# First loads of a fused state-space and gated kernel in another order, with new instruction sequences

## The chip, the core and the metric

The kernel runs on one NeuronCore of a Trainium2 chip. The core has a matrix engine (PE, with its own record PEld for loading weights), a vector engine (DVE), a scalar engine (ACT), a general engine (POOL) and a queue engine (SP), which here issues every DMA. They run side by side and meet only at semaphores. The metric is the device time of one execution in microseconds (us), as the median of several runs; beside it stands one profiled execution with a record of every instruction.

## The reference

```python
def reference(A_u, A_log_A_real, A_A_imag, A_C_real, A_C_imag, A_log_dt, A_D_skip,
              B_x, B_w_gate, B_w_up, B_w_down, gate_w):
    x = A_u                                              # (1, 2048, 448)
    g = _sigmoid((x * gate_w).sum(-1, keepdims=True))
    a = _A_ref(x, ...)   # K = 2 Re(sum_n C P), y = causal convolution of x with K by FFT, + x * D_skip
    b = _B_ref(x, ...)   # (sigmoid(x w_gate) * (x w_up)) w_down, inner width 1792
    return g * a + (1 - g) * b
```

Both branches read the same 2048 tokens of 448 channels. Branch A builds a kernel K of 2048 taps for each channel from 256 complex modes and convolves with it. Branch B is a gated layer with two matrix products up to width 1792 and one down again.

## The kernel before

All work is written as a list of operations in `gated_mix`, each with an engine, operands and a key (engine, tile name, priority). The order on each engine is fixed by hand: the table `PLACE` (lines 28 to 342) gives for every key the positions that its operations take in their engine's sequence. `Plan.order` (line 565 on) merges the five sequences. Every engine then works strictly through its own list: an instruction that waits holds up everything behind it on that engine, and a DMA that waits for a buffer holds up every later DMA on SP.

The parts that matter here:

- **Wake-up.** `step_sizes` memsets a tile `ones` on DVE (L1026) and lets PE multiply it with itself 24 times (L1031, 48 passes in the record, tile `fps`), first of all on PE. Nothing reads the result.
- **Branch B, "GLU".** The tokens come in two halves H and each half in two blocks B of 512. `glu_x` loads a block in four DMAs of 256 KB: column halves z (256 tokens each) times pairs of row blocks k (0 for row blocks 0 and 1, 2 for row blocks 2 and 3). `glu_xk` issues one such DMA into a raw tile (`raw_tile`: 7 buffers `xr0` for the first half, 4 buffers `xr` later), lets ACT round it into `xs` (L1332), and lets DVE compute what rounding lost (L1336, or L1338 and L1339). `glu_w` does the same for the weights of one slice f of 128 gate and 128 up columns: two DMAs (k = 0 and 2), ACT to `wh` (L1365), DVE to `wl` (L1367). A raw buffer comes free when both have read it.
- `glu_mm` multiplies: for one slice f, one block and gate or up (g = 0, 1), 11 matmuls of 512 columns over row blocks 0 to 3 (L1400 to L1405). Row block 0 needs the k = 0 part of the weights and of **both** column halves of x. The result lies in one of two PSUM tiles `gu`. ACT takes the tanh of the gate tile (L1384), DVE multiplies it with the up tile (L1386, to `hh` or `hl`), and these two reads free the PSUM tiles. `glu_down` multiplies with the down weights (L1419, or L1421 to L1423 where the operands are split) and ACT (L1431) or DVE (L1438) adds the result to `ob`.
- **Prologue of branch A.** `step_sizes` and `params` load `x` (log_dt, 1.8 KB), `cr`, `ci`, `la`, `ai` and compute steps and phases, mostly on DVE (L985, L988, L991 are the helper lines).
- **Chunks of branch A.** `kgen` runs 28 chunks; for each, PE computes phases (`tp`, L1224, L1233), ACT takes sines and roundings of them (`cs`, `nn`, L1228 to L1246), DVE multiplies with powers (L1253, L1267, L1270) and PE contracts (`kp`, L1282). GLU matmuls lie between them on PE. Chunk 13 ends the first half of the channels; the same stretch loads the second half H = 1 of the tokens (`xs`, positions 4 to 7 of key ('Act', 'xs', 5)).
- **Convolution** (`Chain`): matmuls on parts of the array (L813, L846, L890, L927), their evacuations `fx` on ACT, and DMAs through DRAM.

The head of the list issues the first loads: `glu_x(0, 0, 0)` and then `glu_w(0, 0, 0)`, so x with all four parts, then the weights of slice 0.

Of the kernel before, what the change touches and what calls it, by code (L numbers as in the profile page):

```python
# [11 lines left out]
F32R = mybir.dt.float32r  # L12
# [16 lines left out]
    ('Act', 'aci', 10): (11, 39,),  # L29
    ('Act', 'aci', 19): (61, 88,),  # L30
    ('Act', 'acr', 10): (15, 37, 46,),
    ('Act', 'acr', 19): (63, 84, 98,),
# [26 lines left out]
    ('Act', 'dots', 1): (28,),  # L59
    ('Act', 'dots', 2): (50,),  # L60
    ('Act', 'dots', 16): (80, 81,),
# [642 lines left out]
def gated_mix(ctx: ExitStack, tc, u, ut, aim, cre, cim, ldt, dskip, gw,  # L704
# [19 lines left out]
    phd = dt_([6, D, N], "phd")  # L724
# [836 lines left out]
```

## Time and profile before

| | us |
|---|---|
| median of 3 runs | 693.52 (692.16 to 694.05) |
| the profiled execution | 693.17 |
| its span | 691.4 |

The span is the time between the first and the last record; 1.8 us of the profiled execution lie outside it. The page of the profile gives the busy time of each engine; a view by windows gives it for chosen stretches, with the granted clock of PE ("PEclk", 1.00 is the full level) and what the DMA engines did. The timeline lists instructions with their start, their duration and, in brackets, how long the engine had sat idle before and what ended that.

### The profile page before, as it was taken

How to read it: one execution, taken by the hardware profiler on the slowest of the kernel's cores; microseconds unless marked ns; L12 is line 12 of the kernel's file. 1: busy time of each engine (PE TensorE's matmuls, PEld its weight loads, DVE VectorE, ACT ScalarE, POOL GpSimd, SP SyncE). 2: the span in 40 equal slices, each digit the busy share in tenths (PEclk: the TensorE clock that was granted, in tenths of full speed). 3: DMA queues.
4: the chain of work that ended last, by engine and by line, in shares of the span. 5: the costliest groups of instructions: out<-in, count | busy, mean ns of one | idle time of the engine just before them, and what ended most of it. 6: DMA issues, size and time to landing. Idle time of an engine off the chain costs nothing.

```text
span 691.4 us, 16303 instructions
## 1 busy us (share of the span) xinstructions
PE 678.0 (98%) x6588; PEld 485.0 (70%) x6588; DVE 603.4 (87%) x705; ACT 513.7 (74%) x934; POOL 276.4 (40%) x280
## 2 busy tenths in 40 slices
PE   8999999999999999999999999999999999999996
PEld 7766667877876687675556667778878766556874
DVE  5999999999999999999999788999973479667976
ACT  5587799899999999999999999999942351342110
POOL 0215458556467758584665745758000000000000
PEclk9999999999999999998999999999999999999999
DMA  9768442646886784859966885355947973879966
GB/s 261 190 161 220 111 125 52 169 118 246 193 172 153 183 201 127 241 169 221 170 167 182 215 230 124 103 210 156 190 104 184 247 254 139 281 251 247 183 171 172
DMA packets 98771, 126.11 MB, mean 182 GB/s; under 512 B 31240, under 2 KB 81096, under 8 KB 97672
## 3 DMA queue, kind: packets, MB, share of 16 engines
q1 hardware_dynamic: 98696, 125.07, 69.2%
q8 instruction: 52, 0.85, 0.5%
q14 instruction: 23, 0.19, 0.1%
HBM read 81.46 MB, written 43.58 MB: 181 GB/s over the span
## 4 chain that ended last, share of the span: by engine, by line
PE 83%; ACT 9%; DVE 3%; DMA 2%; issue 1%; SPq 0%; ACTq 0%; DVEq 0%
PE gu_gps L1400 11%; PE gu_gps L1401 10%; PE gu_gps L1402 10%; PE dn_gps L1419 8%; PE kp_egp L1282 6%; PE dn_gps L1421 4%; PE tp_egp L1224 4%; PE dn_gps L1422 4%; PE dn_gps L1423 4%; PE tp_egp L1233 4%; PE fps_fups L813 3%; PE gu_gps L1404 3%; PE gu_gps L1405 3%; PE fps_fups L846 2%; PE fps_fups L890 2%; PE fps_fkps L890 2%
## 5 line engine op out<-in xcount | busy, mean ns | idle before, releaser
L1400 PE MATMUL gu_gps<-xs_glu,wh_glu 128*128 128x512 f32 x336 | 146.9, 437 | 0.4 <-DVE hh_glu L1386 0.3
L1401 PE MATMUL gu_gps<-xs_glu,wh_glu 128*128 128x512 f32 x336 | 132.4, 394 | 0.0
L1402 PE MATMUL gu_gps<-xs_glu,wl_glu 128*128 128x512 f32 x336 | 132.3, 394 | 0.0
L1270 DVE TENSOR_TENSOR cs_eg<-cs_eg,es_eg 128x2048 f32<-128x2048 f32 x56 | 130.3, 2326 | 1.3
L1214 POOL TENSOR_TENSOR tb_eg<-tb_eg 128x96 f32<-128x96 f32 (+2 forms) x84 | 115.0, 1372 | 5.9
L1253 DVE TENSOR_TENSOR es_eg<-tb_eg 128x1024 f32<-128x1024 f32 x112 | 111.4, 1016 | 2.2
L1400 PEld LDWEIGHTS gu_gps<-xs_glu,wh_glu 128*128 128x128 f32 x336 | 63.5, 189 | 29.7 <-issue 12.6
L1384 ACT ACTIVATE sg_glu<-gu_gps 128x512 f32<-128x512 f32 x56 | 34.0, 607 | 63.5 <-PE gu_gps L1405 60.4
L1267 DVE TENSOR_TENSOR cs_eg<-cs_eg,es_eg 128x1024 f32<-128x1024 f32 x56 | 70.6, 1260 | 10.9 <-ACT cs_eg L1246 7.7
L1230 ACT ACTIVATE nn_eg<-cs_eg 128x512 fp32r<-128x512 f32 x112 | 72.6, 648 | 6.0 <-PE tp_egp L1233 4.6
L1401 PEld LDWEIGHTS gu_gps<-xs_glu,wh_glu 128*128 128x128 f32 x336 | 63.6, 189 | 15.9 <-issue 5.6
L1402 PEld LDWEIGHTS gu_gps<-xs_glu,wl_glu 128*128 128x128 f32 x336 | 63.4, 189 | 15.0 <-DVE wl_glu L1367 0.5
L1217 POOL TENSOR_TENSOR tb_eg<-tb_eg,bs_eg 128x32 f32<-128x32 f32 x84 | 70.4, 841 | 5.8
L1228 ACT ACTIVATE cs_eg<-tp_egp 128x512 f32<-128x512 f32 x112 | 68.6, 618 | 3.2 <-DVE og L958 2.0
L1236 ACT ACTIVATE cs_eg<-tp_egp 128x512 f32<-128x512 f32 x112 | 68.4, 616 | 1.7 <-PE tp_egp L1233 1.5
L1235 ACT ACTIVATE cs_eg<-tp_egp 128x512 f32<-128x512 f32 x112 | 68.2, 618 | 1.5 <-PE tp_egp L1233 1.1
L1438 DVE SCALAR_TENSOR_TENSOR ob_glu<-dn_gps,og,ob_glu 128x448 f32<-128x448 f32 x72 | 48.7, 677 | 23.3 <-PE dn_gps L1423 21.3
L1246 ACT ACTIVATE cs_eg<-cs_eg,half_pi 128x1024 f32<-128x1024 f32 x56 | 66.1, 1180 | 0.5
L1204 POOL MEMSET tb_eg<- 128x96 f32 x28 | 7.8, 286 | 131.6 <-DVE es_eg L1253 124.2
L1282 PEld LDWEIGHTS kp_egp<-cs_eg 128*32 128x32 f32 x3584 | 51.3, 110 | 11.0 <-issue 8.6
L1282 PE MATMUL kp_egp<-cs_eg 128*32 128x64 f32 x3584 | 55.8, 220 | 0.1
L1421 PE MATMUL dn_gps<-vh_glu,hh_glu 128*128 128x448 f32 x136 | 52.3, 384 | 0.8 <-DVE ob_glu L1438 0.8
(161 smaller groups left out, 1338.7 us busy)
## 6 DMA issues: line engine op xcount, KB each, us to landing
shf<-fx_fu SPq DMA_DIRECT2D x16, 896.0 KB
fx_fu<-shf SPq DMA_DIRECT2D x16, 896.0 KB
us<-fx_fu SPq DMA_DIRECT2D x16, 896.0 KB
xr_glu<-in_w_dram SPq DMA_DIRECT2D x52, 256.0 KB
uax_fk<-us SPq DMA_DIRECT2D x16, 448.0 KB
ua_fk<-us SPq DMA_DIRECT2D x16, 448.0 KB
xr_glu<-in_w_dram SPq DMA_DIRECT2D x17, 224.0 KB
gt_pre<-in_u_dram SPq DMA_DIRECT2D x8, 448.0 KB
```

The lines of the kernel that those rows point to most:

```text
L1214: pool(96 * m, lambda n=n, m=m: G.tensor_mul(g3(n + 1, m), g3(1, m), g3(n, 1).to_broadcast([128, 32, 3, m])))
L1217: pool(32, lambda e=e: G.tensor_mul(t(e + 1), t(e), b(3)))
L1228: op("Act", c_act(512, True), lambda: S.activation(cs[:, 1, ds, 32:96], block(tp), AF.Copy, bias=MAGIC), [tp], [(cs, ("s", i))], prio)
L1230: op("Act", c_act(512), lambda: S.activation(block(nn), cs[:, 1, ds, 32:96], AF.Copy, scale=-1.0, bias=MAGIC), [(cs, ("s", i))], [nn], prio)
L1253: V.tensor_mul(o.rearrange("p d (i k) -> p d i k", k=ny), x.unsqueeze(3).to_broadcast([128, 16, nx, ny]), y.unsqueeze(2).to_broadcast([128 ...
L1267: op("DVE", c_dve(1024), lambda: V.tensor_mul(cs[:, :, :, 0:32], cs[:, ::-1, :, 63:31:-1], es[:, :, 0:32].unsqueeze(1).to_broadcast([128, ...
L1270: op("DVE", c_dve(2048), lambda: V.tensor_mul(cs[:, :, :, 32:96], cs[:, :, :, 32:96], es[:, :, 32:96].unsqueeze(1).to_broadcast([128, 2, 1 ...
L1282: T.matmul(kp[32 * j:32 * j + 32, q], cs[:, z, 4 * j + q, 64:96], cs[:, z, 4 * j + q, 0:64], start=cs is parts[0] and z == 0 and q == 0, s ...
L1400: T.matmul(p.real, wh[:, k, cs], x[:, k], start=(k == 0), stop=False)
L1401: T.matmul(p.real, wh[:, k, cs], x[:, 4 + k], start=False, stop=False)
L1402: T.matmul(p.real, wl[:, k, cs], x[:, k], start=False, stop=False)
L1421: T.matmul(p[:, :D], hh[:, ts], vh.real, start=(i == 0), stop=False)
```

## The change

It does two things.

First, `glu_x(0, 0, 0)` and `glu_w(0, 0, 0)` become `glu_first(0)`. The same six loads, with the same roundings behind them, come in the order: x of the first 256 tokens with row blocks 0 and 1; weights of slice 0, row blocks 0 and 1; x of the second 256 tokens, row blocks 0 and 1; then the same three for row blocks 2 and 3. `glu_w` is cut into a generator for that.

```diff
+    def glu_first(prio):
+        x = xs[0, 0] = glu.tile("xs", 2, (128, 7, 512), F32R)
+        parts = glu_w_parts(0, 0, prio)
+        for k in (0, 2):
+            glu_xk(x, k, 0, slice(0, 256), 0, prio)
+            next(parts)
+            glu_xk(x, k, 1, slice(256, 512), 256, prio)
+        for _ in parts:
+            pass
+
...
     def glu_w(H, f, prio):
+        for _ in glu_w_parts(H, f, prio):
+            pass
+
+    def glu_w_parts(H, f, prio):
         wh, wl = (glu.tile(t, WB, (128, 4, 256), F32R) for t in ("wh", "wl"))
...
             glu_split(wr, lambda wr=wr: wr.real, wh, wl, lambda t, k=k: t[:, k:k + 2], k, 512, prio, 7 * H + f // 2)
+            yield
         ws[H, f] = (wh, wl, vh, vl)
...
-    glu_x(0, 0, 0)
-    glu_w(0, 0, 0)
+    glu_first(0)
```

Second, the table `PLACE` is replaced: the sequences of PE, ACT, DVE and SP are new from end to end (POOL's stays). On PE no operation moves by more than 15 positions of 1043. The entries of the head that the text below speaks of:

```diff
-    ('DVE', 'hh', 5): (27, 47, 68, 94, 113,),
-    ('DVE', 'ones', 10): (1,),
-    ('DVE', 'phs', 20): (0,),
-    ('DVE', 'wl', 0): (6, 8,),
-    ('DVE', 'wl', 1): (9, 16,),
-    ('DVE', 'x', 10): (11,),
-    ('DVE', 'xs', 0): (2, 3, 5, 7,),
+    ('DVE', 'hh', 5): (21, 50, 69, 91, 113,),
+    ('DVE', 'ones', 10): (0,),
+    ('DVE', 'phs', 20): (95,),
+    ('DVE', 'wl', 0): (1, 5,),
+    ('DVE', 'wl', 1): (7, 8,),
+    ('DVE', 'x', 10): (10,),
+    ('DVE', 'xs', 0): (2, 3, 4, 6,),
...
-    ('SP', 'ai', 10): (28,),
-    ('SP', 'ci', 10): (6,),
-    ('SP', 'cr', 10): (10,),
-    ('SP', 'x', 10): (8,),
-    ('SP', 'xr0', 1): (7, 9,),
-    ('SP', 'xr0', 2): (11, 12, 14, 15,),
+    ('SP', 'ai', 10): (23,),
+    ('SP', 'ci', 10): (15,),
+    ('SP', 'cr', 10): (8,),
+    ('SP', 'x', 10): (9,),
+    ('SP', 'xr0', 1): (6, 7,),
+    ('SP', 'xr0', 2): (10, 11, 12, 13,),
```

In the PE sequence the first eight GLU steps of slice 0 now go g0 row blocks 0, 1, then g1 row block 0, then g0 row blocks 2, 3, then the rest of g1 (before: all of g0, then all of g1). Around chunk 13 the PE sequences read, from the contraction `kp` 13 to the first GLU step of the second half (`gu` 224):

```
before: kp13, tp116, tp118, dn98, dn99, fps22, tp117, tp119, fps23, tp120, gu224
after:  kp13, fps22, tp116, dn97, tp118, dn98, dn99, fps23, dn100, tp117, dn101, tp119, gu224
```

and `dn97` stands before `kp13` in the sequence before. On ACT the rounding `nn` 58, which `tp` 117 reads, stands 4 positions behind the evacuation of chunk 13 (`ke` 13) before and 9 behind it after; `nn` 59, which `tp` 119 reads, follows 3 positions behind `nn` 58 in both.

## Rows read from the trace of the kernel before

**Rows 1.** Page, part 1: busy us (share of the span) of each engine.

```profile
PE 678.0 (98%) x6588; PEld 485.0 (70%) x6588; DVE 603.4 (87%) x705; ACT 513.7 (74%) x934; POOL 276.4 (40%) x280
```

**Rows 2.** Windows: length, busy us of PE PEld DVE ACT POOL, PEclk, DMA, GB/s.

```profile
20.00:25.00 5.00, 5.00 (x23) 3.91 (x22) 5.00 (x9) 0.58 (x1) 0.00 (x0) 1.00 1.04 274
...
100.00:300.00 200.00, 199.25 (x2467) 149.52 (x2466) 196.47 (x189) 193.17 (x355) 128.05 (x122) 1.00 0.66 166
...
310.00:316.00 6.00, 4.54 (x19) 2.52 (x18) 5.99 (x8) 5.97 (x13) 0.00 (x0) 0.84 0.81 207
316.00:321.00 5.00, 5.00 (x12) 3.32 (x11) 4.97 (x6) 4.33 (x8) 2.71 (x4) 0.51 0.93 249
321.00:350.00 29.00, 27.19 (x388) 17.05 (x390) 27.50 (x25) 27.01 (x47) 20.18 (x19) 1.00 0.95 183
...
500.00:680.00 180.00, 179.56 (x1207) 124.23 (x1207) 128.40 (x161) 55.84 (x106) 0.00 (x0) 1.00 0.75 206
```

**Rows 3.** Windows, wake-up line L1031 alone: PE, PEld, PEclk, DMA share, GB/s.

```profile
1.60:6.80 5.20, 5.12 (x24) 5.12 (x25) 1.00 0.89 272
6.90:9.50 2.60, 2.60 (x25) 2.60 (x24) 1.00 1.06 313
```

**Rows 4.** Timeline of the first 17 us: start, duration, engine, line, operation [idle before].

```profile
0.91 0.48 DVE L1184 MEMSET phs<- 1x512 f32 x1 [0.91 <-PEq L1551]
1.46 0.17 DVE L1026 MEMSET ones_pro<- 112x128 f32 x1
...
1.68 8.10 PE L1031 MATMUL fps_fups<-ones_pro 112*128 112x128 f32 x48 [1.68 <-DVE ones_pro L1026]
...
5.76 0.63 ACT L1332 ACTIVATE xs_glu<-xr_pre 128x512 fp32r<-128x512 f32 x1 [0.97 <-DMA xr_pre<-in_ut_dram]
...
8.62 0.63 ACT L1365 ACTIVATE wh_glu<-xr_pre 128x512 fp32r<-128x512 f32 x1 [2.23 <-DMA xr_pre<-in_w_dram]
...
9.54 0.47 PE L1400 MATMUL gu_gps<-xs_glu,wh_glu 128*128 128x512 f32 x1
...
9.68 0.62 ACT L1365 ACTIVATE wh_glu<-xr_pre 128x512 fp32r<-128x512 f32 x1
...
10.34 0.42 DVE L1339 TENSOR_TENSOR xs_glu<-xr_pre,xs_glu 64x256 fp32r<-64x256 f32 x1
...
12.65 0.16 DVE L985 TENSOR_SCALAR xr_pro<-x_pro 112x4 f32<-112x4 f32 x1
...
13.02 0.39 PE L1400 MATMUL gu_gps<-xs_glu,wh_glu 128*128 128x512 f32 x1
...
14.83 0.39 PE L1400 MATMUL gu_gps<-xs_glu,wh_glu 128*128 128x512 f32 x1
...
15.88 0.69 DVE L1386 SCALAR_TENSOR_TENSOR hh_glu<-sg_glu,gu_gps 128x512 f32<-128x512 f32 x1
15.97 0.39 PE L1402 MATMUL gu_gps<-xs_glu,wl_glu 128*128 128x512 f32 x1
...
16.62 0.50 PE L1400 MATMUL gu_gps<-xs_glu,wh_glu 128*128 128x512 f32 x1 [0.27 <-DVE hh_glu L1386]
```

**Rows 5.** Timeline of PE around a step on a part of the array (L813).

```profile
141.93 1.03 PE L813 MATMUL fps_fups<-fx_fu,ft_fu 64*128 64x224 f32 x8
142.89 0.50 PE L1404 MATMUL gu_gps<-xs_glu,wh_glu 128*128 128x512 f32 x1
143.22 0.39 PE L1405 MATMUL gu_gps<-xs_glu,wl_glu 128*128 128x512 f32 x1
```

**Rows 6.** Timeline of PE around chunk 13.

```profile
312.88 0.50 PE L1233 MATMUL tp_egp<-nn_eg,idn 128*128 128x512 f32 x1 [1.00 <-ACT nn_eg L1230]
...
316.64 0.63 PE L1400 MATMUL gu_gps<-xs_glu,wh_glu 128*128 128x512 f32 x1
317.07 0.63 PE L1401 MATMUL gu_gps<-xs_glu,wh_glu 128*128 128x512 f32 x1
```

**Rows 7.** Chain of work that ended last, in order of time: start, us, what.

```profile
34.32 1.50 PE dn_gps L1419 x4
```

More of the change, by code (lines that the diff above doesn't have):

```diff
@@ L28 @@
 PLACE = {
[L29 to L32, printed above, removed]
[26 rows of a table removed]
-    ('Act', 'dots', 1): (28,),
-    ('Act', 'dots', 2): (50,),
-    ('Act', 'dots', 16): (80, 81,),
[15 rows of a table removed]
+    ('Act', 'aci', 10): (14, 37,),
+    ('Act', 'aci', 19): (63, 88,),
+    ('Act', 'acr', 10): (12, 35, 47,),
+    ('Act', 'acr', 19): (64, 84, 97,),
[26 rows of a table added]
+    ('Act', 'dots', 1): (29,),
+    ('Act', 'dots', 2): (48,),
+    ('Act', 'dots', 16): (65, 82,),
[15 rows of a table added]
         911, 914, 916,),
[2 rows of a table removed]
[2 rows of a table added]
     ('Act', 'idn', 10): (17,),
-    ('Act', 'junk', 10): (34, 59,),
-    ('Act', 'junk', 19): (76, 78, 113,),
[12 rows of a table removed]
-    ('Act', 'pos_sb', 10): (65, 74,),
[22 rows of a table removed]
-    ('DVE', 'aci', 10): (50,),
-    ('DVE', 'aci', 19): (105,),
-    ('DVE', 'acr', 10): (82,),
+    ('Act', 'junk', 10): (33, 59,),
+    ('Act', 'junk', 19): (75, 79, 114,),
[12 rows of a table added]
+    ('Act', 'pos_sb', 10): (69, 71,),
[22 rows of a table added]
+    ('DVE', 'aci', 10): (42,),
+    ('DVE', 'aci', 19): (110,),
+    ('DVE', 'acr', 10): (85,),
     ('DVE', 'acr', 19): (150,),
@@ L123 @@
     ('DVE', 'ai', 19): (145,),
[13 rows of a table removed]
-    ('DVE', 'dtp', 10): (40,),
-    ('DVE', 'dtv', 10): (26,),
[14 rows of a table removed]
-    ('DVE', 'half_pi', 0): (4,),
[21 rows of a table removed]
[13 rows of a table added]
+    ('DVE', 'dtp', 10): (44,),
+    ('DVE', 'dtv', 10): (32,),
[14 rows of a table added]
+    ('DVE', 'half_pi', 0): (25,),
[21 rows of a table added]
     ('DVE', 'og', 1): (52,),
     ('DVE', 'og', 2): (80,),
[1 row of a table removed]
-    ('DVE', 'ones', 10): (1,),
-    ('DVE', 'p', 10): (18, 20, 21, 22, 23, 24, 25,),
-    ('DVE', 'phs', 20): (0,),
[6 rows of a table removed]
-    ('DVE', 'skip', 20): (35,),
[6 rows of a table removed]
-    ('DVE', 'uax', 40): (540, 544, 551, 552, 567, 565, 576, 575, 582, 581, 588, 587, 594, 595, 600, 599, 629, 630,
[26 rows of a table removed]
[1 row of a table added]
+    ('DVE', 'ones', 10): (0,),
+    ('DVE', 'p', 10): (16, 18, 20, 24, 27, 28, 30,),
+    ('DVE', 'phs', 20): (95,),
[6 rows of a table added]
+    ('DVE', 'skip', 20): (13,),
[6 rows of a table added]
+    ('DVE', 'uax', 40): (544, 542, 550, 551, 567, 566, 576, 574, 579, 582, 588, 587, 594, 595, 598, 599, 629, 630,
[26 rows of a table added]
         1032, 1035, 1038, 1039, 1042,),
     ('PE', 'fps', -1): (0,),
[43 rows of a table removed]
[43 rows of a table added]
     ('Pool', 'bsx1', 10): (5, 11,),
```

494 rows, old and new, of the table PLACE are left out of this document.

## Prediction, made before the changed kernel was run

> **What bounds the kernel now.** I read the page first, then the windows, then the timeline of the first 17 us. PE is busy for 98% of the span [rows 1], and the windows show why that is a bound: from 100 to 300 us it is busy in 199.25 of 200 us, from 500 to 680 us in 179.56 of 180 us, while in the latter ACT has 55.84 us of work [rows 2]. So whatever time PE loses anywhere is paid at the end, unless something else than PE sets the pace there. Two places do set another pace. At the head PE waits for loads, and DVE is full (5.00 of 5.00 us from 20 to 25 us). Around chunk 13, from 310 to 316 us, PE has only 4.54 of 6 us to do, because ACT is full (5.97 of 6), and directly after it the granted clock stands at 0.51, so PE ran at its lower level of 1.2 GHz instead of 2.4 [rows 2]. From 100 to 300 us DVE (196.47) and ACT (193.17 of 200) are close behind PE: time that PE gains at the head can turn into waits for ACT there.
>
> The timeline of the head shows a point that decides most of this case. The wake-up passes keep PE from 1.68 to 9.78 us, and the first GLU matmul starts at 9.54, as they drain [rows 4]. Loads that come earlier cannot start it before the wake-up ends.
>
> **The change, part by part.**
>
> *(a) The wake-up starts earlier.* On DVE the memset `ones` goes ahead of the memset `phs`, which took its 0.48 us first: `ones` started at 1.46, `phs` at 0.91 [rows 4], so the passes start 0.55 us earlier, at 1.13. They are not all alike: 24 of them fill 5.12 us (0.213 each), then 25 fit in 2.60 us (some 0.11 each) [rows 3]. PEclk reads 1.00 in both rows, but the passes tell that the first ones ran at half rate, until shortly before 6.9 us. If the rise moves along with the start, PE is free 0.55 us earlier. If it comes at the same moment, 0.55/0.213 = 2.6 more passes run slowly and as many quick ones fall away: 2.6 x 0.11 = 0.29 us. I take -0.4, between -0.55 and -0.29. The Trainium skill ("TensorE: Matmul & The Clock Gate", section "What you observe") says that the rise moves by some 500 ns from run to run; by that (an estimate) the wake-up's end would scatter by about a quarter of a microsecond in either kernel, so this term is the least sure to be seen in a single profile.
>
> *(b) The first slice.* Landings can be bounded by ACT's waits: the third load had landed by 5.76, the fifth by 8.62, the sixth by 9.68 [rows 4]. Before, PE's first matmul needs the fifth load. After, it needs the third: 5.76 plus ACT's 0.63 plus DVE's 0.69 (as L1386, 512 columns) [rows 4] is 7.1 us, two microseconds ahead of the wake-up's end near 9.1. So the new load order buys nothing for the first matmul. It buys what comes behind it: before, the 22 matmuls of slice 0 took 14.83 - 9.54 = 5.29 us; eight matmuls without a stall took 14.83 - 13.02 = 1.81, or 0.226 each [rows 4], so 22 would take 4.98, and 0.3 us were stalls. After, nine matmuls (2.0 us) need only row blocks 0 and 1, until about 11.1; the sixth load, at 9.68, is rounded by 10.3 and its remainder ready by about 11.1 (two DVE steps of 0.42, as L1339). That just fits. I take -0.25, between -0.3 and 0.
>
> *(c) The wait at 16.6.* Slice 1's up tile waits until DVE has done L1386 (15.88, 0.69 us): matmul starts 15.97 and 16.62 are 0.65 apart instead of 0.23, and 0.1 us goes to the restart [rows 4]. In the new DVE sequence L1386 stands at position 21 instead of 27, with 12 small steps of 0.16 us between the load of `x` and it. `x` is now the tenth DMA instead of the ninth; All 7 raw buffers are taken when the eighth load is due, so SP waits until DVE has finished with the first; DVE's list now puts a `wl` step of 0.69 us ahead of that. So SP's wait is that much longer, and `cr`, `x` and the second block of x queue behind it. The DMA engines have a backlog then (a DMA share of 1.06 up to 9.5 us [rows 3]) which hides most of it. I expect `x` near 12.8 instead of 12.65, L1386 at 14.8 to 15.3, and PE there at 9.1 + 28 x 0.226 = 15.4. -0.4, between -0.5 and 0.
>
> *(d) DVE keeps the `phs` memset*, at position 95, about 47 us. There it lies in a full stretch: 0 to +0.48; PE has GLU steps in hand then, so +0.1.
>
> Head together: -0.95, at the ends -1.35 and +0.2. Two things lie between that and the end of the kernel. PE's list is fixed, so a microsecond won at 16 us is a microsecond by which PE comes too early to the first chunk of branch A, whose ACT and DVE chain starts no earlier by itself (`ci` goes from position 6 to 15 on SP, `ai` only from 28 to 23). Some of it becomes waiting for ACT. I count -0.7.
>
> *(e) The new sequences.* Reading both PE lists, PE changes between full and partial array shapes 178 times before and 175 times after. The first full matmul behind a partial step takes 0.33 instead of 0.23 us [rows 5]: 0.1 us per change, -0.3 in all. POOL keeps its list. All other moves reach 15 positions of 1043 at most.
>
> *(f) Chunk 13.* Here the order does matter. `tp` 119 waits 1.00 us for ACT [rows 6]. After, PE has three more steps ahead of `tp` 117 (`dn` 97 and `dn` 100 at two of the passes of which four take 1.50 us [rows 7], and `fps` 23, about 1 us from the first to the next step [rows 5]: 2.5 us), but on ACT the rounding that it waits for stands nine instead of four places behind `ke` 13, and at 5.97/13 = 0.46 us each [rows 2] that is another 2.3 us. That cancels. Between `tp` 117 and `tp` 119 a `dn` (0.75 us) is new while ACT has the same three steps: the wait of 1.00 falls to some 0.4. -0.6, between -1.2 and +0.6.
>
> Sum: -0.7 - 0.3 - 0.6 = -1.6 against the profiled execution's 693.17, or 691.6. That execution is 0.35 below the median of the three runs, and I put the forecast at 691.7. Its own range goes from 690.3 to 693.8 by the ends named.
>
> **The rivals.**
>
> *The half-clock stretch goes.* A PEclk of 0.84 over 6 us means 2 x 0.16 x 6 = 1.9 us at half rate, 0.51 over the next 5 us means 4.9: for 6.8 us matmuls start 0.43 us apart (316.64, 317.07) instead of 0.226 [rows 2, 4, 6]. What ran then would have taken half the time: at most 3.4 us are lost, less what PE would have waited for ACT anyway; I take 2.8. If the fuller order of (f) keeps the clock up, the time is 691.7 - 2.8 = 688.9 (688.2 to 690). For it: the `dn` steps fill the emptiest part. Against it: ACT is full, so the waits are not gone.
>
> *The head's gain is swallowed.* By the Trainium skill ("Perfetto Trace Analysis", section "Identifying the Most-Contended Engine") PE's matmul busy share is no good measure, and its weight-load share is: 70% [rows 1], below DVE's 87%. By that, DVE would be the engine to watch. As a mechanism here: the prologue of branch A is a chain on DVE, which is full; it gets `x` no earlier, and the 0.48 us of `phs` as well. Then the first chunks come when they did, PE waits for ACT what it had won, and only (e) and some of (f) are left: 692.7 to 694.5, about 693.3. Against it: PE's waits in the long stretch are under 1 us of 200 [rows 2], and PE alone fills the end. The load order could also do nothing because the wake-up covers it; that gives the same time.
>
> *A second half-clock stretch.* Slower by one mechanism: the new sequences leave PE short of work at another place, and the clock falls there too. The likeliest place is 321 to 350 us, where PE already idles 1.8 of 29 us with ACT at 27.01 [rows 2]. It decides where PE's idle time comes as dense as before chunk 13's end, some 1.5 us within 6. Price: 1.5 us of idle time plus up to 3.4 of half rate, some 4.6: 696.3.
>
> **How the numbers follow.** The forecast 0.42, the half-clock stretch gone 0.30, the gain swallowed 0.14, a second stretch 0.14. A measurement of this kernel tells about 0.3% from no change, 2.1 us: under 691.44 is faster, over 695.6 slower. Faster: the 0.30, and a quarter of the forecast's range, 0.40 together. Within 0.3%: three quarters of the forecast and the swallowed gain, 0.45. Slower: 0.15. The range goes from 688.4 to 694.6; it leaves out the second stretch and the outermost end of the case without one.
>
> **What the profile of the changed kernel would show.** (a) `ones` at 0.91, the first pass at 1.1, the first GLU matmul near 9.1; if it stands at 9.5, the rise of the clock did not move. (b) No gap in slice 0, its 22 matmuls in 5.0 us. (c) No wait of PE behind L1386 near 15.5. (d) PE's waits for ACT's `nn` between 60 and 300 us as few as before; more of them means that the gain was swallowed. (f) PEclk around chunk 13, and anywhere else below 1.00. The prediction would be wrong if `x` or the second block landed well after 13 us, or if the profile shows waits on DVE in the first 60 us that the old one does not have.

## The result and the profile after

| | us, median (lowest to highest) | profiled execution | its span |
|---|---|---|---|
| before, 6 runs | 693.78 (692.16 to 694.96) | 693.17 | 691.4 |
| changed, 6 runs | 696.96 (694.96 to 698.24) | 696.97 | 695.2 |

The ratio is 1.0047, with a 95% interval from 1.0028 to 1.0066: the changed kernel is slower by about 3.2 us. The forecast was 691.7, with a range up to 694.6.

(TensorE, VectorE, ScalarE and SyncE are the engines that the rows call PE, DVE, ACT and SP. A "record" is one pass of a matmul in the profile.)

The page, its part 1, then TensorE's row of part 2 (40 slices of 17.4 us), then two rows of part 3 (packets, MB, share of the DMA engines):

```profile
PE 678.0 (98%) x6588; PEld 485.0 (70%) x6588; DVE 603.3 (87%) x705; ACT 512.6 (74%) x934; POOL 277.3 (40%) x280
...
PE   9999999999999999998999999979999999999996
...
q1 hardware_dynamic: 98696, 125.07, 69.8%
q8 instruction: 52, 0.85, 0.5%
```

The busy sums are those of [rows 1] to within 1.1 us, so no engine got more to do. What is new is the digit 7 in the 27th slice, 452 to 469 us, a stretch in which the kernel before shows a 9. The last row, which the prediction did not use, says that TensorE's own code also comes in by DMA, in 52 pieces of 16 KB.

**The head came out better than forecast in this profile.** Timeline of the first 16 us (columns as in [rows 4]):

```profile
0.83 0.17 DVE L1026 MEMSET ones_pro<- 112x128 f32 x1 [0.83 <-PEq L1565]
...
1.05 7.96 PE L1031 MATMUL fps_fups<-ones_pro 112*128 112x128 f32 x48 [1.05 <-DVE ones_pro L1026]
...
8.77 0.48 PE L1415 MATMUL gu_gps<-xs_glu,wh_glu 128*128 128x512 f32 x1
...
11.84 0.16 DVE L985 TENSOR_SCALAR xr_pro<-x_pro 112x4 f32<-112x4 f32 x1
...
13.86 0.39 PE L1415 MATMUL gu_gps<-xs_glu,wh_glu 128*128 128x512 f32 x1
14.09 0.39 PE L1416 MATMUL gu_gps<-xs_glu,wh_glu 128*128 128x512 f32 x1
14.13 0.69 DVE L1401 SCALAR_TENSOR_TENSOR hh_glu<-sg_glu,gu_gps 128x512 f32<-128x512 f32 x1 [0.54 <-PE gu_gps L1420]
14.32 0.39 PE L1417 MATMUL gu_gps<-xs_glu,wl_glu 128*128 128x512 f32 x1
```

(The GLU lines stand 15 further down: L1415 is L1400 of before, L1401 is L1386.) The first GLU matmul starts at 8.77 instead of 9.54, slice 0 ends at 13.86 instead of 14.83, and at 14.13 VectorE waits for TensorE, no longer the other way round [rows 4].

**The loss is in one place.** The contraction (`kp`, L1282: a block of 128 small matmuls for each chunk) serves as a ruler. Its 28 blocks stand in the same order in both kernels, and those shown here stand at the same place among TensorE's records or up to five records away, which is about a microsecond at most. Starts read from the two traces:

```
contraction          0      3     13     16     23     24     27    span
before          116.08 163.42 306.11 349.17 451.56 466.17 508.32   691.4
changed         113.80 162.51 304.50 347.58 449.53 469.81 512.10   695.2
difference       -2.28  -0.91  -1.61  -1.59  -2.03  +3.64  +3.78    +3.8
```

The gain of the head shrinks and grows on the way (over all blocks up to 23 it lies between 0.30, at contraction 5, and 2.28 us), and it is still there at 449 us. Between contractions 23 and 24 it is lost with 5.67 us, and little happens afterwards. TensorE in the kernel before, then in the changed kernel, with the one row of ScalarE that waited longest (timeline):

```profile
451.56 1.99 PE L1282 MATMUL kp_egp<-cs_eg 128*32 128x64 f32 x128
```

```profile
448.57 1.03 PE L813 MATMUL fps_fups<-fx_fu,ft_fu 64*128 64x224 f32 x8
449.53 1.92 PE L1282 MATMUL kp_egp<-cs_eg 128*32 128x64 f32 x121
455.44 0.32 PE L1282 MATMUL kp_egp<-cs_eg 128*32 128x64 f32 x7 [4.00 <-issue]
...
456.23 0.60 ACT L1228 ACTIVATE cs_eg<-tp_egp 128x512 f32<-128x512 f32 x1 [3.97 <-PE tp_egp L1224]
...
457.14 0.57 PE L1436 MATMUL dn_gps<-vh_glu,hh_glu 128*128 128x448 f32 x1
457.52 0.58 PE L1437 MATMUL dn_gps<-vh_glu,hl_glu 128*128 128x448 f32 x1
```

After 121 of the 128 matmuls of the block TensorE stands for 4.00 us ("the hole" below), and the releaser is "issue": it waited for nothing that the profile shows. ScalarE waits for TensorE, so it isn't the cause. The windows over the same stretch (columns as in [rows 2]), of before and then of the changed kernel:

```profile
448.00:450.00 2.00, 2.00 (x11) 1.67 (x10) 1.97 (x2) 1.97 (x5) 1.92 (x2) 1.00 0.55 202
450.00:452.00 2.00, 2.00 (x40) 1.43 (x42) 1.90 (x2) 2.00 (x5) 2.00 (x2) 1.00 0.22 88
```

```profile
446.00:448.00 2.00, 2.00 (x10) 1.65 (x9) 2.00 (x2) 2.00 (x6) 1.92 (x2) 1.00 0.44 149
448.00:450.00 2.00, 2.00 (x43) 1.34 (x45) 1.41 (x3) 2.00 (x6) 1.92 (x2) 1.00 1.03 416
450.00:452.00 2.00, 1.45 (x104) 1.28 (x92) 1.87 (x2) 1.97 (x4) 1.84 (x4) 1.00 1.01 355
452.00:454.00 2.00, 0.00 (x0) 0.00 (x0) 1.97 (x3) 0.26 (x1) 0.81 (x2) 1.00 0.75 242
...
456.50:459.90 3.40, 3.40 (x10) 2.82 (x9) 1.40 (x2) 2.36 (x5) 0.00 (x0) 0.50 0.18 40
```

The hole is 4.00 us; behind it the granted clock stands at 0.50 (1.2 GHz of 2.4) for 3.4 us. What each costs is read from the experiments below. Five of their profiles have a shorter hole here (0.32 to 3.08 us) and no half clock behind it, and all of them take the length of their hole plus 14.89 or 14.90 us from contraction 23 to 24; the one with the same list there and no hole takes 14.64 (before: 14.61). So of the 5.67 us the hole is 4.00, starting again behind it 0.25, and the half clock 1.4. The DMA engines are full from 448 us on, which SyncE's timeline explains:

```profile
447.10 0.81 SPq L713 DMA_DIRECT2D shf<-fx_fu  x2
448.01 0.85 SPq L713 DMA_DIRECT2D xr_glu<-in_w_dram  x1
```

Two stores of 896 KB and a weight load are issued within a microsecond. In the kernel before these stores stood six places apart in SyncE's list and were issued at 450.87 and 460.95; in the new list they are neighbours. The DMA queues, first from 447 to 453 us, then from 453 to 455 us:

```profile
q1 hardware_dynamic: 292, 1.85, 84.9%
...
q1 hardware_dynamic: 141, 0.24, 33.2%
q8 instruction: 1, 0.02, 2.9%
```

No piece of code arrived from 447 to 453 us. Piece 36 (counted from 0) starts at 453.18 by its record, takes 0.94 us, and TensorE goes on at 455.44. In the kernel before the same piece started at 448.56.

### The profile page after: what moved, and what is told of

The parts are those of the page before. It is cut to its first block, busy times and chain, and to the rows that moved or that the text cites. A ratio compares the mean times of both kernels' runs of the same rounds, so it can differ in the third digit from the quotient of the medians.

```text
span 695.2 us, 16300 instructions
## 1 busy us (share of the span) xinstructions
PE 678.0 (98%) x6588; PEld 485.0 (70%) x6588; DVE 603.3 (87%) x705; ACT 512.6 (74%) x934; POOL 277.3 (40%) x280
## 4 chain that ended last, share of the span: by engine, by line
PE 76%; ACT 12%; DVE 6%; issue 3%; DMA 2%; SPq 0%; ACTq 0%; DVEq 0%
PE gu_gps L1415 9%; PE gu_gps L1416 8%; PE gu_gps L1417 8%; PE dn_gps L1434 6%; PE kp_egp L1282 6%; PE dn_gps L1436 4%; PE tp_egp L1233 4%; PE dn_gps L1437 4%; PE dn_gps L1438 4%; PE tp_egp L1224 3%; PE gu_gps L1419 3%; PE fps_fups L813 3%; PE gu_gps L1420 3%; ACT cs_eg L1246 2%; PE fps_fups L846 2%
## 5 line engine op out<-in xcount | busy, mean ns | idle before, releaser
L1415 PE MATMUL gu_gps<-xs_glu,wh_glu 128*128 128x512 f32 x336 | 144.2, 429 | 0.7 <-DVE sg_glu L1404 0.4
L1415 PEld LDWEIGHTS gu_gps<-xs_glu,wh_glu 128*128 128x128 f32 x336 | 63.7, 190 | 30.7 <-issue 14.6
L1217 POOL TENSOR_TENSOR tb_eg<-tb_eg,bs_eg 128x32 f32<-128x32 f32 x84 | 72.9, 871 | 5.8
L1282 PEld LDWEIGHTS kp_egp<-cs_eg 128*32 128x32 f32 x3584 | 51.5, 110 | 15.0 <-issue 12.3
L1282 PE MATMUL kp_egp<-cs_eg 128*32 128x64 f32 x3584 | 56.2, 220 | 4.0 <-issue 4.0
L1233 PE MATMUL tp_egp<-nn_eg,idn 128*128 128x512 f32 x112 | 51.8, 463 | 4.1 <-ACT nn_eg L1230 3.7
```

The costliest lines, as they stand in the source:

```text
L1217: pool(32, lambda e=e: G.tensor_mul(t(e + 1), t(e), b(3)))
L1233: op("PE", c_mm(532), lambda: T.matmul(tp.real, idn.real, nn.real, start=False, stop=True, skip_group_check=True), [nn, idn], [tp], prio)
L1282: T.matmul(kp[32 * j:32 * j + 32, q], cs[:, z, 4 * j + q, 64:96], cs[:, z, 4 * j + q, 0:64], start=cs is parts[0] and z == 0 and q == 0, s ...
L1415: T.matmul(p.real, wh[:, k, cs], x[:, k], start=(k == 0), stop=False)
```

## The experiments

Theory C: TensorE ran dry of instructions, because piece 36 waited in the DMA engines behind the burst; 121 small matmuls in 1.92 us use up the stock faster than anything else in this kernel. Theory D: a wait for data, a bank or an engine that the profile doesn't name. Theory S: no single place, the new order is slower in general. Each ratio below is to runs of the kernel before on the same chip (medians there 692.15 to 693.49); SP's list is the table that sets the order of its DMAs.

**One store away from the burst.**

```
 SP list of the changed kernel, positions 242 to 246
-shf 1, shf 0, xr 9, phs 26, xr 10
+shf 1, xr 9, phs 26, xr 10, shf 0
```

> The changed kernel, but the second of its two neighbouring stores of x to shf (896 KB each, issued together at 447.10 us) stands four places later in SP's order. Theory C (TensorE ran out of instructions: its own 16 KB instruction transfer waited in the DMA engines behind the two stores and a weight load, 448 to 453.2 us): one store fewer takes about 2.2 us off the queue (896 KB at the 416 GB/s of that stretch), so the instruction transfer starts near 451.0, and the hole of 4.00 us shrinks to about 1.8 us: 693.3 to 694.8 us. Theory D (the hole is a wait for data, an operand, a PSUM bank or a late engine, and has nothing to do with instructions): the store isn't read before 480 us, so the hole stays at 4 us and the time at 697. Theory S (no single place: the new order is slower in many places): 697, whatever happens to the hole.

Measured: 694.86 us, ratio 1.0011 [0.9993, 1.0029]. TensorE in contraction 23 (timeline):

```profile
450.29 1.92 PE L1282 MATMUL kp_egp<-cs_eg 128*32 128x64 f32 x121
454.59 0.32 PE L1282 MATMUL kp_egp<-cs_eg 128*32 128x64 f32 x7 [2.39 <-issue]
```

The hole shrinks from 4.00 to 2.39 us, though the store that moved is read by nothing here (the two loads and `phs` behind it come one place earlier). Against D and S. No half clock follows this hole.

**Both stores away.**

```
-shf 1, shf 0, xr 9, phs 26, xr 10
+xr 9, phs 26, xr 10, shf 1, shf 0
```

> The changed kernel, but both neighbouring stores to shf stand behind the weight load that now follows contraction 23, so that none is in flight at 447 to 453 us. Theory C: the instruction transfer starts within 2 us of 447, the hole is gone, and with it the half-clock stretch of 456.5 to 459.9 us: 697.0 - 4.0 - about 1.6 = 691.4 us (691 to 692.5), faster than both kernels. Theory D: the hole stays or moves, 695 to 697. Theory S: a hole gone and still about 695.5 or more.

Measured: 692.16 us, ratio 0.9987 [0.9971, 1.0002].

```profile
450.07 1.92 PE L1282 MATMUL kp_egp<-cs_eg 128*32 128x64 f32 x121
452.59 0.32 PE L1282 MATMUL kp_egp<-cs_eg 128*32 128x64 f32 x7 [0.60 <-issue]
```

Two entries of one list take away 4.8 us by the medians, 4.2 by the ratios. The break stays at the same matmul, the 122nd, with 0.60 us: piece 36 comes at 450.20, still somewhat late, though the DMA engines have little to do by then (a share of 0.92 from 446 to 448 us, 0.13 from 448 to 450).

**The borders of the pieces moved, the DMAs as they were.**

```
-WAKE = 24
+WAKE = 32
```

> The changed kernel with 32 wake-up matmuls in place of 24, nothing else: every later instruction of TensorE stands 32 places (16 matmul records) further back in its stream, and the borders of the 16 KB pieces fall 16 records earlier in the program; all DMAs keep their order. Price at the head: 16 more records at 0.10 us = 1.7 us. Theory C: the piece that came late is asked for some 4 us earlier, about 443 us, when the DMA engines are nearly idle; no hole in contraction 23: 697.0 + 1.7 - 5.6 = 693.1 us (692.5 to 694.5). Theory D: the burst and the data are as before, so the hole of about 4 us stays: 698.7 us. Theory S: 698.7 us.

Measured: 696.96 us, ratio 1.0048 [1.0029, 1.0066]; theory C had 693.1. The hole in contraction 23 is gone as it said, and three others have opened, each behind a late piece (this is TensorE's timeline in contraction 16):

```profile
352.22 1.87 PE L1282 MATMUL kp_egp<-cs_eg 128*32 128x64 f32 x117
355.92 0.41 PE L1282 MATMUL kp_egp<-cs_eg 128*32 128x64 f32 x11 [1.83 <-issue]
```

Here piece 26 starts at 353.14 us, with the DMA engines full just before (1.16 from 350 to 352 us); the second, 1.49 us at 270.5 us, follows piece 18 at 269.38. The third, 0.87 us at 150.7 us in contraction 2, follows piece 6 at 149.34, and there the DMA engines are at 0.11 to 0.54. The three add up to 4.2 us. The expectation failed because it took one border into account, and the edit moves them all.

**Only the first loads and operations in the new order.** The lists of the changed kernel for the first 17 DMAs, 30 operations of TensorE, 23 of ScalarE and 111 of VectorE; the lists of before behind them.

> Only the first loads and the first operations of each engine in the new order (17 DMAs of SP, 30 operations of TensorE, 23 of ScalarE, 111 of VectorE); all that follows is in the order of the kernel before. Theory C: the gain of the head (1.5 to 1.9 us at equal work, as the changed kernel has it from 21 to 449 us) arrives at the end, since the stores stand apart there: 692.0 us (691.2 to 692.8). Theory S, that the gain of the head is given back along the way: 693.3 to 694. Where the new order of the loads is itself what costs: 695 or more.

Measured: 702.50 us, ratio 1.0129 [1.0102, 1.0156]. TensorE waits for the other engines at six places of 1.1 to 2.6 us between 27 and 70 us (2.58 for VectorE's `rt` at 67.07); the kernel before has one there, of 1.07. The clock then stands at 0.50 for 6.8 us from 67.9. The two halves don't fit together; this run doesn't price the head. At the point in question it has before's order and no hole.

**Only the rest in the new order.** Before's lists up to 108 DMAs and 127 operations of TensorE, the changed lists from there.

> The loads and the first part of the kernel before (127 operations of TensorE, 123 of ScalarE, 136 of VectorE, 108 DMAs: up to about 80 to 165 us, by engine), and the order of the changed kernel from there on. Theory C: the hole belongs to the new order at 447 us and not to the new loads, so it is here too, 2.5 to 4.5 us long in contraction 23: 693.0 + 4.0 + 1.0 = 698 us (696.5 to 699). Were it tied to the loads at the start: no hole, 693.

Measured: 702.74 us, ratio 1.0159 [1.0123, 1.0194].

```profile
457.62 1.88 PE L1282 MATMUL kp_egp<-cs_eg 128*32 128x64 f32 x120
461.26 0.32 PE L1282 MATMUL kp_egp<-cs_eg 128*32 128x64 f32 x8 [1.76 <-issue]
```

The hole is there without the new loads, but of 1.76 us, under what was expected; the seam brought waits of its own here as well (1.20 us for VectorE at 113.58, 1.51 for a load at 146.95), and its profile has half-clock stretches at three places, so only the place of the hole can be read from this run, not a price.

**A burst in the kernel before.**

```
 SP list of before, behind the load of ft at 445 us
+jk 0, jk 1, jk 2        (896 KB each, DRAM to DRAM, read by nobody)
```

> The kernel before with three copies of 896 KB from one DRAM tensor to another added to SP's list behind the load of ft at 445.48 us; nobody reads them. Theory C (TensorE's instruction transfer queues behind whatever fills the DMA engines): it came at 448.6 us in the kernel before; now it waits for 2.7 MB and two weight loads, to about 455 us, and TensorE, which uses up its stock at 453.3 us in the middle of contraction 23, stands for 2 to 5 us there with no releaser: 693.0 + 3 to 6 (hole and half-clock stretch) = 696 to 699 us. Theory D (a wait for data): a copy that nobody reads can only delay the weight loads behind it, which are needed some 10 us later or more: 693 to 694 us, and no hole in contraction 23.

Measured: 694.90 us, ratio 1.0038 [1.0023, 1.0053], but not by the hole. Piece 36 starts at 446.67, before the copies fill the engines, and contraction 23 runs through. The loss is a wait for data:

```profile
461.32 0.47 PE L1226 MATMUL tp_egp<-pos_sb,phs 97*128 97x512 f32 x1 [1.76 <-DMA phs<-phd]
```

**A longer burst, earlier.** Eight copies in place of three, placed to start at 436 us.

> The kernel before, with eight copies of 896 KB from one DRAM tensor to another behind the load of fx at 436 us, read by nobody: the DMA engines are full from 438 us to about 455 (7.2 MB at the 416 GB/s seen there). The three copies of the earlier run came just behind the instruction transfer of 446.7 us; these are there before it. Theory C: the transfer starts near 455, TensorE stands in contraction 23 at its record 4773 (452 to 453 us) for 3 to 5 us with no releaser, and the end is 4 to 7 us later: 696 to 699.5 us. Rival (instruction transfers don't wait for data): it starts at 446 to 449, no hole in contraction 23, only waits for data that came late (phs, ft or weights, 1.8 us in the earlier run): 694 to 696.

Measured: 706.37 us, ratio 1.0210 [1.0190, 1.0230]; more than expected, and for another reason. Piece 36 starts at 449.56, while the engines are full (DMA share 1.00 from 448 to 452 us) and stay so for many microseconds: it isn't kept until the burst ends, as the expectation had it, and lies nearer to the rival's 446 to 449 us. So theory C is wrong in the form that the piece waits for the whole burst; that it is delayed by a burst at all rests on the runs with the stores, and on the next one. Contraction 23 runs through, and TensorE then waits 11.49 us for the load of `ft` behind the copies. Against the run with three copies the piece came 2.9 us later; in this order it has about 3 us to spare.

**Other bytes in the place of the stores.**

```
 SP list with both stores moved, behind fx 5 at 445 us
+jk 0, jk 1, jk 2        (896 KB each, DRAM to DRAM, read by nobody)
```

> The kernel with both stores moved (692.16 us), and three copies of 896 KB from one DRAM tensor to another at the place in SP's list that the stores had left; nobody reads them, and all other orders and the code stay. SP reaches them at 445 us, so the DMA engines are full from about 447 to 453. In the runs so far that have this order of contraction 23, TensorE's idle time in it was the start of instruction piece 36 after the contraction's own start, plus 0.35 to 0.5 us (start +3.65 us: 4.00; +2.05: 2.39; +1.27: 1.76; +0.13: 0.60). Theory C: the piece starts 1.5 to 3 us into the contraction, the hole is back with 2 to 3.5 us and no releaser, and the time is 692.2 + 2 to 4.5 = 694 to 697 us. Rival (the stores, or their waits, are what matters, not the load on the DMA engines): piece 36 starts within 0.3 us of the contraction, the hole stays at 0.6 us, 692 to 693 us.

Measured: 695.58 us, ratio 1.0046 [1.0029, 1.0063].

```profile
450.02 1.92 PE L1284 MATMUL kp_egp<-cs_eg 128*32 128x64 f32 x121
455.02 0.32 PE L1284 MATMUL kp_egp<-cs_eg 128*32 128x64 f32 x7 [3.08 <-issue]
```

The hole is back at the same matmul, and most of the loss with it. So it is the load on the DMA engines, not the stores and not what waits for them. No half clock follows here either.

All runs that leave the borders of the pieces in place, some of them told of below, by the start of piece 36 against the start of contraction 23 (from the records of the instruction transfers and of L1282):

```
kernel                                   piece minus contraction    TensorE dry for
3 copies in before                              -3.77                   0
before                                          -3.00                   0
new order in the head only                      -2.70                   0
8 wake-up matmuls of 128 x 4                    -1.06                   0
8 copies in before                              -0.92                   0
both stores moved, gap of chunk 15 filled       -0.14                   0.32
both stores moved                               +0.13                   0.60
8 wake-up matmuls of 4 x 4                      +0.18                   0.60
new order in the rest only                      +1.27                   1.76
one store moved                                 +2.05                   2.39
both stores moved, 3 copies in their place      +2.47                   3.08
changed kernel                                  +3.65                   4.00
```

Where TensorE ran dry, it stood for the delay plus 0.34 to 0.61 us, in every kernel. That settles theory C for this hole. The delay itself has two parts: against before (-3.00) the changed list without the burst has the piece at -1.06 to +0.18, in four profiles, and the burst adds some 3.5 us to that (3.65 against 0.13). In the old order the piece comes some 3 us ahead of the block, and there the eight copies delay it without a hole.

**A shorter wake-up.**

```
 both stores moved
-WAKE = 24
+WAKE = 16
```

> The kernel with both stores moved (692.16 us), and 16 wake-up matmuls in place of 24. The wake-up ends at 8.8 us there, the first loads are ready by about 7.1 us. Theory C with the head bound by the wake-up: 16 matmul records at 0.10 us = 1.7 us less, 690.5 us, if no border of a 16 KB piece of instructions falls behind a burst; the borders stand 16 records later in the program, so contraction 23 lies wholly inside one piece, but others move as well, and each new hole would be read in the trace as an idle time of TensorE without a releaser (1.2 to 4 us each). Rival, the head is bound by the loads as soon as the wake-up is shorter: 691.5 to 692.2 without any such hole.

Measured: 699.25 us, ratio 1.0106 [1.0090, 1.0122]. The head is faster (first GLU matmul at 6.51 us), and the kernel slower:

```profile
181.82 0.40 PE L1417 MATMUL gu_gps<-xs_glu,wl_glu 128*128 128x512 f32 x1
185.95 0.58 PE L1233 MATMUL tp_egp<-nn_eg,idn 128*128 128x512 f32 x1 [3.73 <-issue]
```

Between 165.9 and 182.9 us no piece of code started; with both stores moved and 24 matmuls one started at 176.1. The DMA engines are full from 178 to 182 us in this run (0.92 and 1.16).

**The same with the length of the code kept.** The 8 matmuls that the wake-up lost stay, with 4 columns each. In a first version only the columns of the moving operand were cut:

```
-for _ in range(WAKE):
-    T.matmul(wake[:, :128], ones.real, ones.real, ...)
+for k in range(WAKE):
+    n = 128 if k < 16 else 4
+    T.matmul(wake[:, :n], ones.real, ones[:, :n], ...)
```

> As the run with 16 wake-up matmuls, but the other 8 stay in the program with 4 columns in place of 128, so that TensorE's stream keeps its length and every border of a 16 KB piece its place. Theory C (the hole of 3.73 us at 182.2 us of that run came of the shifted borders): no hole at 182 us and none in contraction 23; against the kernel with both stores moved, what the shorter wake-up left of its gain at 160 us there (-1.08 against -0.54 us at equal work): 692.2 - 0.5 = 691.6 us (690.8 to 692.2). Rival (that hole came of the earlier start of the work, at which other transfers meet): the hole is here again, and 698 to 699 us.

Measured: 691.34 us, ratio 0.9987 [0.9974, 0.9999]. No hole at 182 us, but the wake-up wasn't shortened (8.15 us for its 48 passes, the first GLU matmul at 9.06; the passes of 4 columns start 0.112 us apart, as those of 128 do): this doesn't tell the rivals apart, and the time repeats the one with both stores moved. In a second version the weights are cut to 4 columns as well, `T.matmul(wake[:n, :n], ones[:, :n], ones[:, :n], ...)`:

> As the run before with 16 full wake-up matmuls and 8 of 4 columns, but these 8 now load only 4 columns of weights too (4 x 4 in place of 128 x 4; a matmul of 4 columns took as long as one of 128 there, 0.07 us a pass, so that the wake-up was not shortened). The stream keeps its length and every border of a 16 KB piece its place. Theory C (the hole of 3.73 us at 182 us of the run with 16 wake-up matmuls came of the shifted borders): the first GLU matmul starts near 7 us as there, and there is no hole at 182 us: about 0.5 us under the kernel with both stores moved, a ratio of 0.998 to the kernel before (0.9965 to 0.9995). Rival (the hole came of the earlier start of the work): a hole at 180 to 184 us again, ratio 1.008 to 1.011. Rival (8 passes of 4 columns take as long whatever the weights): first GLU matmul at 8.8 to 9.1 us, ratio 0.9987.

Measured: 691.35 us, ratio 0.9975 [0.9959, 0.9992], the fastest kernel of this study against before, on the same chip. (The expectation's 0.07 us a pass is a misreading; it was 0.112.) Timeline of the head, and the windows from 180 us:

```profile
1.05 6.05 PE L1032 MATMUL fps_fups<-ones_pro 112*128 112x128 f32 x48 [1.05 <-DVE ones_pro L1026]
7.03 0.49 PE L1416 MATMUL gu_gps<-xs_glu,wh_glu 128*128 128x512 f32 x1
...
180.00:182.00 2.00, 2.00 (x32) 1.41 (x20) 2.00 (x3) 1.97 (x5) 0.67 (x2) 1.00 1.16 192
182.00:184.00 2.00, 2.00 (x10) 1.66 (x10) 2.00 (x3) 1.90 (x4) 0.00 (x0) 1.00 0.91 165
```

The work starts 0.52 us later than with 16 matmuls and 1.74 earlier than in the changed kernel (some 0.5 us of that is the clock, which rose at 4.73 us in this profile and at 5.97 in the changed kernel's), the DMA engines are as full (1.16), a piece started at 175.3, and there is no hole. So the place of the borders made that hole, as far as two starts 0.52 us apart allow one to say. The two kernels differ in 8 matmuls that compute nothing anyone reads, and in their ratios by 1.3%, of which the hole at 182 us with the half clock behind it (0.50 from 186 to 188 us) is the largest single part.

**The gap in chunk 15.** The changed kernel has the half-clock stretch of [rows 2] in another place (windows; the first row answers to 310 to 316 us of [rows 2]):

```profile
310.00:316.00 6.00, 5.66 (x24) 3.50 (x24) 5.95 (x8) 6.00 (x12) 0.00 (x0) 1.00 0.85 199
...
326.80:330.20 3.40, 3.19 (x7) 2.44 (x8) 3.37 (x4) 3.00 (x6) 2.84 (x2) 0.50 1.05 213
...
100.00:300.00 200.00, 199.39 (x2471) 149.79 (x2470) 195.97 (x189) 191.78 (x353) 129.49 (x122) 1.00 0.68 171
```

It begins in a wait of 1.21 us for ScalarE's `nn` (325.80 to 327.00 us). Two swaps fill that gap:

```
 both stores moved
 TensorE:  -tp 127, gu 230     +gu 230, tp 127
 ScalarE:  -cs 219, nn 63      +nn 63, cs 219
```

> The kernel with both stores moved (692.16 us), and two swaps at the gap of 1.21 us that TensorE has at 326.1 to 327.3 us there, waiting for ScalarE's nn: a GLU group of three matmuls goes ahead of the tp matmul that waits, and ScalarE's nn ahead of the sine beside it. Theory K (the gap is what the half clock of 327 to 330 us follows on, as the prediction's rival had it): the gap goes (-1.2 us) and the half clock with it (about 1.7 us of 3.4 us at half rate): 689.3 us (688.8 to 690). Rival: the gap goes, the clock falls nevertheless: 691.0. Rival: the next wait takes its place (ScalarE has no slack there): 692.2.

Measured: 693.49 us, ratio 1.0008 [0.9995, 1.0021]. Windows of the same stretch, of this run:

```profile
326.80:330.20 3.40, 2.35 (x8) 0.99 (x6) 3.33 (x3) 3.40 (x6) 3.24 (x3) 1.00 0.99 203
```

The clock stays up in this profile, TensorE is busy for 2.35 us, where it was 3.19 at half rate in the changed kernel, and ScalarE is full. The next wait (1.28 us at 330.65, again for `nn`) remains. But the swaps can't be given the credit for the clock. The run with 8 wake-up matmuls of 4 x 4 has both stores moved and no swap, its profile has the same gap (1.20 us), the same second wait (1.28), and no half clock:

```profile
327.00:330.50 3.50, 2.34 (x8) 1.04 (x6) 3.47 (x4) 3.40 (x7) 2.82 (x4) 1.00 1.15 194
```

The runs with 32 and with 16 wake-up matmuls show the same; six other profiles with this order and gap do have the half clock. So the gap alone does not decide whether the clock falls, and theory K is not shown. At equal clock the swaps are worth 0.14 us (13.06 us from contraction 14 to 15, against 13.20 to 13.21 in those three). The profile is not typical of its kernel either: its execution took 691.65 us; seven of the twelve have a lower mean clock (0.993 to 0.996) and a median of 693.84 us.

The kernel before itself shows what the stretch costs. The run with three copies has before's order there, and its profile has no clock below 1.00 from 311 to 334 us. The window of 314 to 321 us, of before and then of that run:

```profile
314.00:321.00 7.00, 6.74 (x17) 4.49 (x17) 6.96 (x8) 6.30 (x12) 2.71 (x4) 0.51 0.90 243
```

```profile
314.00:321.00 7.00, 5.30 (x21) 3.33 (x21) 6.96 (x8) 6.93 (x14) 2.62 (x4) 1.00 0.94 254
```

From contraction 13 to 16 it took 43.06 us with the half clock and 41.88 without: 1.2 us. TensorE at full rate waits for ScalarE (6.93 of 7 us) for most of what the half clock had cost. The runs of the kernel before beside the experiments agree with that price: 51 of the 92 have a mean clock of 0.994 and a median of 693.24 us, 24 have 0.999 and 692.06.

## Why the prediction was wrong

- **(a) The wake-up: right in the mechanism, a little small.** `ones` at 0.83, passes from 1.05, 0.63 us earlier; the first GLU matmul came 0.77 earlier; counted were 0.4, at most 0.55. The two single profiles leave much to chance, about the quarter of a microsecond either way that the prediction allowed for: with the new start the clock rose anywhere from 5.80 to 6.93 us and the first GLU matmul came at 8.68 to 9.22 (six profiles with the full wake-up of 24), with the old start at 5.79 to 7.99 and 9.08 to 10.05 (four). The middle values of the two groups lie 0.7 us apart, near the 0.63 of the start.
- **(b) The first slice: right.** 22 matmuls in 13.86 - 8.77 = 5.09 us; forecast 5.0, before 5.29.
- **(c) The wait at 16.6: right in the result, wrong in a detail.** The wait is gone. `x` was in use at 11.84 us, where 12.8 was expected: the longer wait on SyncE did not delay it. Two new waits for VectorE, 0.17 us each at 29.98 and 42.62, are the sign that was to count against the prediction; they are too small to matter.
- **(d) `phs`** was set at 59.83 us, where about 47 was expected; what it cost can't be read separately.
- **The head as a whole and the swallowed gain.** Counted were 0.7 us at the end; the contractions show 0.3 to 2.3 along the way and 2.03 at contraction 23, and TensorE's waits from 100 to 300 us are no more than before (199.39 busy against 199.25 [rows 2]). That rival, with 0.14, did not come about, and VectorE, the engine that it would watch, did not set the pace. With the burst taken away, what is left at the end is about 0.9 us by the medians (ratio 0.9987, interval up to 1.0002, so it is not clear of zero). The list without the burst loses another 0.9 us of the lead between contractions 23 and 24 (15.50 us from one to the other, 14.61 before): that is its break of 0.60 us and the start behind it, for the run with this list and no break takes 14.64.
- **(e) The new sequences: this is the step that failed.** It priced them by TensorE's changes of array shape alone (-0.3) and set all other moves at nothing, since "all other moves reach 15 positions of 1043 at most". That holds for TensorE alone: operations move by up to 56 of 382 places on SyncE, 26 of 917 on ScalarE and 95 of 681 on VectorE. (The changes of shape, counted by the steps `fps` and `kp` in the lists, are 169 and 161, not 178 and 175; at 0.1 us each that is no matter.) A move of six places on SyncE put two stores of 896 KB side by side, 2.4 us ahead of the only kind of block that uses up a piece of code in 2 us, in an order of TensorE in which the piece comes late anyway: +5.7 us. Nothing in the sum had TensorE's code as a user of the DMA engines, though part 3 of the page names its queue. The pieces of before alone would not have told it: 16 of the 52 start with the DMA engines full (a share of 0.95 or more in the 1.5 us ahead), without harm; it takes a dense block as well.
- **(f) Chunk 13: the mechanism came, the gain didn't.** The wait of 1.00 us is gone and 310 to 316 us is fuller (5.66 instead of 4.54 us), but chunk 15 has a wait of 1.21 us and the half clock instead. From contraction 12 to 15, which hold the same 501 records in both: 42.59 before, 42.33 after, each with a half-clock stretch; forecast -0.6. Without one the new order is the slower of the two: 41.13 to 41.16 us for the old (the runs with copies and the one with the head alone), 42.03 for the new (8 matmuls of 4 x 4, 32 matmuls). ScalarE sets the pace there, as "what bounds the kernel now" says, and the step didn't hold on to it.
- **The half-clock stretch goes (0.30): the price was the wrong term.** 2.8 us were counted for it; 1.2 were measured. The waits for ScalarE that it hides were set at 0.6 us and are 2.2 (3.4 - 1.2). At 1.2 this case is 690.5 us, inside the forecast's own range, and no rival of its own.
- **A second half-clock stretch (0.14)** gave 696.3 us, and 696.96 was measured; but it stood at 321 to 350 us and came from lack of work. In the changed kernel a second stretch did follow, at 456.5 us, behind a hole that had nothing to do with work or with waits between engines. The sign and the size agree by luck; the mechanism that it names did not bring them about.

What was to show it: "PEclk anywhere else below 1.00" was the right sign to name, and it leads to 456 us.

How the wait comes about is told by the Trainium skill ("Runtime: NRT & Kernel Launch", section "Instruction fetch mechanics"): an engine's sequencer fetches its code by its own DMA queue in blocks of 16 KiB, and crossing a border is mostly hidden. This case agrees in the size (52 pieces of 16 KB) and shows where it isn't hidden: 4.00 us. The same section says that the next block is fetched while the current one executes. That agrees too: piece 37 started 11 matmuls after piece 36 had come into use, so about one piece lay ready. The skill also says ("DMA: Bandwidth & Descriptors", section "Queues, rings and completion order") that a DMA engine takes turns between its queues packet by packet; that a piece started in the midst of the eight copies agrees. That it still came 2.9 us later there than with three copies, and 3.5 us later behind the stores than without them, is not explained by it. What that delay is made of stays open, and so does why the piece comes about 3 us ahead of contraction 23 in the old order and beside it in the new one even with the DMA engines nearly idle.

## What to carry to other kernels

A long unrolled program has one more stream on the DMA engines, its own code, and an order that brings the data earlier can starve it: look for idle time with no releaser in the middle of a run of small matmuls, and read the code queue's transfers beside it. Keep large stores from landing together just ahead of such a run; and after any change of the number of TensorE's instructions, however early and however idle, go through all borders again, since they all move. Price a half-clock stretch only by what TensorE would have done at full clock, which beside a full ScalarE was less than half of the loss that the clock alone suggests (1.2 of 3.4 us). And before an edit is given the credit for a clock that stays up, compare several executions without the edit.

## What the runs showed of the hardware that was not expected

- A delay of one 16 KB instruction transfer by 3.65 us past the start of a block stopped TensorE for 4.00 us, and the clock then stood at 0.50 for 3.4 us: 5.7 us in all for a transfer that takes 0.94.
- A block of 128 matmuls with 64 columns uses up its instructions in 1.99 us; 128 matmuls of 512 columns, at 0.226 each, need 29 us for as many. A hole can also open a few matmuls behind such a block, when the border lies there (3.73 us at 182.2 us with 16 wake-up matmuls, 1.49 at 270.5 with 32).
- A pass of 4 columns on 128 columns of weights took as long as one of 128 columns (0.112 us from start to start for either), while one of 4 columns on 4 columns of weights took 0.025.
- Whether the clock falls at chunk 13 differs between executions of the same order (0.51 in one profile, 1.00 in two others), which alone is 1.2 us of scatter.
- A hole did not always bring the half clock with it: it followed those of 4.00, 3.73 and 1.76 us, and not those of 3.08, 2.39 and 1.83.
